# A radix-2 stage of a long convolution taken from TensorE: folds on VectorE and GpSimd, and real and imaginary parts on partitions

## The chip, the cores and the metric

One core of one Trainium2 chip runs the whole kernel. The metric is device time in microseconds. The kernel before takes 373.03 us, the median of 3 runs (372.75 to 373.64).

## The reference

Two branches work on the layer-normalised query `xn` and are added to `x`. Sizes: S = 2048 positions, D = 448 channels, F = 1792.

```python
# A: a 4-tap shift of k, times v, then a causal convolution of length S per channel
k_shift = sum over t of k_pad[:, t:t + S, :] * shift_k[:, 3 - t]
kv = k_shift * v
y = irfft(rfft(pad(kv, 2 * S)) * rfft(pad(ssm_k, 2 * S)))[:S] + kv * ssm_D
A = xn * y
# B: dense -> Mish -> dense
B = mish(xn @ w1 + b1) @ w2
out = x + A + B
```

All operands are fp32. The convolution is computed as a transform in three stages: 64 points with a fold, then 32 points, a product in the frequency domain, and the two stages back.

## The kernel before, in words

**The dense branch is the backbone.** The positions are cut into 8 chunks of 256, the F columns into 7 pairs of 128-wide tiles. Each of the 56 (chunk, pair) steps has two slots. The even slot holds the first product (`g1_mm`, 22 matmuls of 256 columns), the odd slot Mish on ScalarE and its split in two parts on VectorE (`mish`; the tile `acl` is the low part), and the second product (`g2_mm`, 12 matmuls of 448 columns) of the pair two steps back. Layer norm of the next chunk runs beside it: statistics on VectorE in small pieces (`dv` drips one behind another instruction), the normalised rows (`xn`, L391) on GpSimd.

**The transform is laid between the slots by hand.** `at(slot, f)` puts `f` ahead of a slot's dense work, `after(slot, f)` behind it; the lists are run in order of slots, and every engine executes its instructions in the order in which they were written. There is no other scheduler. A DMA is issued by the sequencer of the engine that it is written for, in that engine's order, and what stands behind it on that queue waits as long as it waits.

**Stage 1** (slots 0 to 63) takes 16 groups, 8 of the filter H and 8 of kv: `f1_mm` does 8 matmuls, `f1_fold` adds and subtracts, `f1_out` writes to the DRAM scratch `Dh` or `Dkv`. For kv, `taps` forms the shifted product on VectorE, and one of four multiplications goes to GpSimd (`taps_pool`, L154).

**Stage 2** (slots 63 to 90) takes the frequencies in 8 octets of 8, with three slots to an octet. For octet `o`: `o_load` reads `ah` and `av` from the scratch (one buffer each, so that the load of octet o+1 waits for the matmuls of octet o); `f2_mm` transforms H (`h2_mm`) and kv (`v2_mm`), each with 16 matmuls of a 64-row, 32-column part of the array; ScalarE copies the results out of PSUM (`hs`, `vs`); `prod` multiplies the two complex numbers with six VectorE instructions; `i1_mm` does the first step back with 16 matmuls of a 32-row, 64-column part; ScalarE copies (`qe`) and issues two writes to the scratch `E`. fp32 matmuls are two instructions each, so a view counts 32 where the code has 16.

**Stage 3** (slots 92 to 115) loads `E` by chunks (`e_load`, issued by GpSimd), adds and subtracts halves (`fold`), does the last 8 matmuls of a chunk (`i2_mm`) and gates with the normalised query (`gate`). The first `i2_mm` needs all octets, since every chunk of `E` has rows of every octet. The tables `OCT_AT` and `I2_AT` hold the slots; in stage 2 kv's matmuls stand at 65 + 3 o, H's one slot ahead, `i1_mm` four slots behind.

## Time and profile before

| | |
|---|---|
| median of 3 runs | 373.03 us |
| span of the profiled execution | 370.5 us |
| TensorE busy | 361.2 us, 98% |
| VectorE, ScalarE, GpSimd busy | 261.4, 165.9, 71.2 us |
| DMA traffic | 79.35 MB, 214 GB/s on average |
| stage 2's matmuls (L207 / L250) | 27.9 / 15.8 us of TensorE |

The profile is of one execution, and its span covers the program's instructions from the first to the last; the profiler gives no other time for that execution. The median is 2.5 us above the span. PE is TensorE, PEld its weight loads, DVE VectorE, ACT ScalarE, POOL GpSimd, and SP the queue that issues most loads. A busy TensorE is not one at its peak: matmuls are pipelined, and a part of the array that stands idle doesn't show. The time of a small matmul is read from the distance between its start and the start of what comes behind it.

### The profile page before, as it was taken

Reading aid. Unit: us, or ns where it says so; the run is one execution under the profiler, and the core shown is the slowest. Engines: PE = TensorE matmul, PEld = TensorE weight load, DVE = VectorE, ACT = ScalarE, POOL = GpSimd, SP = SyncE. Lnnn points to the kernel's source line nnn. Section 1 sums busy time; section 2 is a strip of 40 time slices with the busy share of each in tenths; the row PEclk is TensorE's granted clock in tenths of the full one; section 3 lists DMA queues with packets and bytes.
Section 4 is the critical chain, followed back from the end, with each engine's and each line's share of the span. In section 5 each row is a group of like instructions: output and inputs, shape, how many; then the busy total and the mean of one; then the engine's idle time right before and its main releaser. Section 6 shows DMA issues by size and latency. Waiting matters only on the chain.

```text
span 370.5 us, 7467 instructions
## 1 busy us (share of the span) xinstructions
PE 361.2 (98%) x3128; PEld 292.2 (79%) x3128; DVE 261.4 (71%) x358; ACT 165.9 (45%) x277; POOL 71.2 (19%) x59
## 2 busy tenths in 40 slices
PE   8999999999998999999999999999999999999995
PEld 2889888888887988988886666666666879889885
DVE  4899748999968987996435647654474842997751
ACT  2785642343423333343353556555475533235450
POOL 2107002722070223520014000060000005102020
PEclk9999999999999999999999999999999999999999
DMA  8999968757596428504876498988494475949655
GB/s 307 319 308 355 382 233 233 215 159 239 145 294 184 104 58 262 179 25 99 264 235 216 135 282 239 272 271 237 134 328 110 105 239 207 407 195 293 102 69 129
DMA packets 31442, 79.35 MB, mean 214 GB/s; under 512 B 2865, under 2 KB 18098, under 8 KB 31410
## 3 DMA queue, kind: packets, MB, share of 16 engines
q1 hardware_dynamic: 19826, 44.35, 35.4%
q10 hardware_dynamic: 9248, 22.61, 23.0%
q0 software_dynamic: 2336, 11.93, 11.3%
q8 instruction: 24, 0.39, 0.4%
q14 instruction: 8, 0.07, 0.0%
HBM read 50.44 MB, written 28.44 MB: 213 GB/s over the span
## 4 chain that ended last, share of the span: by engine, by line
PE 62%; DVE 4%; ACT 2%; ACTq 1%; issue 1%; DVEq 0%
PE pg L446 24%; PE pg L471 8%; PE pg L473 8%; PE pg L472 8%; PE pc L207 7%; PE pc L250 3%; PE pc L307 2%; PE pc L124 1%; PE pg L406 1%; ACTq L261 1%; ACT a L454 1%; DVE x L171 1%; DVE yc L240 1%; DVE qt L478 0%; ACT XH L418 0%
## 5 line engine op out<-in xcount | busy, mean ns | idle before, releaser
L454 ACT ACTIVATE a<-pg,b1t 128x256 f32<-128x256 f32 x112 | 47.1, 472 | 101.4 <-PE pg L446 80.6
L446 PE MATMUL pg<-XH,w1h 128*128 128x256 f32 x448 | 91.2, 285 | 0.7 <-ACT XH L418 0.7
L446 PEld LDWEIGHTS pg<-XH,w1h 128*128 128x128 f32 x448 | 69.5, 188 | 18.1 <-issue 15.7
L471 PE MATMUL pg<-w2h,ach 128*128 128x448 f32 x224 | 83.0, 371 | 0.0
L472 PE MATMUL pg<-w2l,ach 128*128 128x448 f32 x224 | 81.4, 363 | 0.6 <-DVE w2l L74 0.6
L473 PE MATMUL pg<-w2h,acl 128*128 128x448 f32 x224 | 81.4, 363 | 0.0
L74 DVE TENSOR_TENSOR acl<-a,ach 128x512 fp32r<-128x512 f32 x56 | 38.8, 692 | 55.2 <-ACT ach L73 55.0
L446 PE MATMUL pg<-XL,w1h 128*128 128x256 f32 x448 | 69.6, 277 | 0.0
L446 PEld LDWEIGHTS pg<-XL,w1h 128*128 128x128 f32 x448 | 59.4, 188 | 0.1
L446 PE MATMUL pg<-XH,w1l 128*128 128x256 f32 x336 | 56.9, 278 | 0.0
L471 PEld LDWEIGHTS pg<-w2h,ach 128*128 128x128 f32 x224 | 42.0, 187 | 11.6 <-issue 9.4
L446 PEld LDWEIGHTS pg<-XH,w1l 128*128 128x128 f32 x336 | 46.8, 188 | 0.1
L472 PEld LDWEIGHTS pg<-w2l,ach 128*128 128x128 f32 x224 | 42.1, 188 | 3.5 <-DVE w2l L74 1.1
L473 PEld LDWEIGHTS pg<-w2h,acl 128*128 128x128 f32 x224 | 42.1, 188 | 2.5
L387 POOL TENSOR_TENSOR rstd<-ve,mhalf 128x2 f32<-128x2 f32 (+1 forms) x9 | 8.5, 945 | 162.6 <-DVE ve L384 105.8
L73 ACT CAST ach<-a 128x512 fp32r<-128x512 f32 x56 | 34.7, 620 | 1.8
L154 POOL TENSOR_TENSOR x<-kr,skb 128x896 f32<-128x896 f32 x8 | 17.0, 2129 | 74.9 <-DVE x L153 54.1
L171 DVE TENSOR_TENSOR x<-x 128x896 f32<-128x896 f32 x24 | 26.6, 1107 | 5.1 <-POOL x L154 4.4
L391 POOL TENSOR_SCALAR xn<-qt,mv,rstd 128x448 f32<-128x448 f32 x12 | 26.7, 2231 | 0.6
L418 ACT CAST XH<-pg 128x512 fp32r<-128x512 f32 x16 | 9.4, 587 | 38.7 <-PE pg L406 35.5
L416 DVE TENSOR_TENSOR XL<-pg,XH 128x512 fp32r<-128x512 f32 x16 | 10.9, 687 | 15.5 <-ACT XH L418 15.3
L130 ACT COPY st<-pc 128x896 f32<-128x896 f32 x16 | 14.5, 908 | 14.7 <-PE pc L124 12.8
(71 smaller groups left out, 401.1 us busy)
## 6 DMA issues: line engine op xcount, KB each, us to landing
Dh<-st ACTq DMA_DIRECT2D x16, 448.0 KB, 6.0
Dkv<-st ACTq DMA_DIRECT2D x16, 448.0 KB, 5.1
ah<-Dh SPq DMA_DIRECT2D x8, 896.0 KB, 6.8
av<-Dkv SPq DMA_DIRECT2D x8, 896.0 KB, 5.9
E<-qe ACTq DMA_DIRECT2D x16, 448.0 KB, 5.4
e<-E POOLq DMA_DIRECT2D x8, 896.0 KB, 7.7
kr<-in_k_dram SPq DMA_DIRECT2D x10, 448.0 KB, 6.2
kr<-in_w_dram SPq DMA_DIRECT2D x7, 512.0 KB, 6.3
```

The costliest lines, as they stand in the source:

```text
L73: nc.scalar.copy(h, raw)
L74: V.tensor_sub(l, raw, h)
L130: nc.scalar.copy(st[:, 1], o)
L154: nc.gpsimd.tensor_mul(o, KR[g - u // 2], skb[:, u:u + 1].to_broadcast([128, 2, D]))
L171: V.tensor_add(KV[g], KV[g], o)
L207: nc.tensor.matmul(p[32 * t:32 * t + 32, r, :D], g[rs, t, c], a[rs, t], start=True, stop=True, tile_position=(64 * r, 32 * t))
L391: eng.tensor_scalar(xn[:, jj, :D], Q[c][:, jj], mv[:, j, 0:1], rstd[:, j:j + 1], op0=ALU.subtract, op1=ALU.mult)
L446: nc.tensor.matmul(ps[:, n], l, r, start=n_ == 0, stop=n_ == len(mm) - 1)
L454: nc.scalar.activation(a[:, n], ps[:, n], AF.Mish, bias=b1t[:, 2 * p + n:2 * p + n + 1])
L471: nc.tensor.matmul(ps, ah[:, n, cs], w2h[:, f], start=f == 0, stop=False)
L472: nc.tensor.matmul(ps, ah[:, n, cs], w2l[:, f], start=False, stop=False)
L473: nc.tensor.matmul(ps, al[:, n, cs], w2h[:, f], start=False, stop=f == NF - 1)
```

## The change

Stage 2's 32-point step is cut into a radix-2 stage outside TensorE and two 16-point matmuls.

- **Layout.** A group's results now lie as 32 frequency rows x 2 parts, real and imaginary parts alternating on the partitions. `f1_out` writes four pieces of 32 partitions rather than two of 64, half of them from SP's queue (the last of kv all from ScalarE's). `o_load` reads 2 x 2 x 448 floats to a partition; for octets 4 to 7 (the mirrored frequencies) it exchanges the partitions of the second half, which makes three DMAs of one.
- **`f2_fold`** forms sum and difference of the two halves ahead of the matmuls. kv's folds are on VectorE; H's are on VectorE for octets 0 and 1, on GpSimd from octet 2 on. From octet 4 on the half has a sign by partition: on VectorE this is a `scalar_tensor_tensor`, for GpSimd ScalarE multiplies by the sign first.
- **`f2_mm`** has 16 matmuls as before, each of a 32-row, 32-column part of the array, so that 16 parts rather than 8 are addressed.
- **`h2_turn`** copies H's result from `hs` to `ht` with exchanged partitions, two DMAs of 448 KB on SP's queue.
- **`prod`** has four VectorE multiplications in place (`hs` becomes v times h, `vs` becomes v times the exchanged h), without the sum and the difference: `i1_mm` adds them in its accumulation, with 32 matmuls of 32 x 32 rather than 16 of 32 x 64.
- **`i1_fold`** adds on VectorE and subtracts on GpSimd (both on VectorE for octet 7); **`i1_store`** writes to `E` from SP's queue with four DMAs, from octet 4 on with twelve. Before, ScalarE issued two.
- **`fold`** of stage 3 has four instructions of 448 columns rather than two of 896, two of them `scalar_tensor_tensor`.
- **Slots.** An octet has 3.5 slots on average: kv's matmuls at 66, 70, 73, 77, 80, 84, 87, 91, H's one slot behind those of the octet ahead, `i1_mm` two slots behind kv's. The last `i1_mm` moves from slot 90 to 93, the first `i2_mm` from 98 to 101, the last stays at 110.

```diff
-OCT_AT = (65, 3)
-I2_AT = {98: (6, 7), 102: (0, 1), 106: (2, 3), 110: (4, 5)}
+V_AT = (66, 70, 73, 77, 80, 84, 87, 91)
+I2_AT = {101: (6, 7), 104: (0, 1), 107: (2, 3), 110: (4, 5)}
...
     def f1_out(dst, g, key):
         st = ST.pop((key, g))
+        dst = dst.rearrange("(h k) (r n c) b d -> n c (k r) h (b d)", h=2, r=4, c=2)
         for jj in range(2):
-            nc.scalar.dma_start(dst.rearrange("(h p) n d -> p h n d", h=2)[:, :, 4 * g + 2 * jj:4 * g + 2 * jj + 2].rearrange("p h n d -> p h (n d)"),
-                                st[64 * jj:64 * jj + 64].rearrange("p h b d -> p h (b d)"))
+            for c in range(2):
+                p = 64 * jj + 32 * c
+                (nc.scalar if c or (g, key) == (NO - 1, "kv") else nc.sync).dma_start(dst[2 * g + jj, c], st[p:p + 32].rearrange("p h b d -> p h (b d)"))
...
+    def f2_fold(d, o, name, eng):
+        a = d[o]
+        x = t2([128, 2, D], name)
+        a0, a1 = a[:, :, 0], a[:, :, 1]
+        if o < 4:
+            eng.tensor_add(x, a0, a1)
+            eng is V and dv()
+            eng.tensor_sub(a1, a0, a1)
+            eng is V and dv()
+        elif eng is V:
+            V.scalar_tensor_tensor(x, a1, sg[0], a0, op0=ALU.mult, op1=ALU.add)
+            dv()
+            V.scalar_tensor_tensor(a1, a1, sg[1], a0, op0=ALU.mult, op1=ALU.add)
+            dv()
+        else:
+            nc.scalar.mul(a1, a1, sg[0])
+            eng.tensor_add(x, a0, a1)
+            eng.tensor_sub(a1, a0, a1)
+        d[o] = x, a1
...
+    def f2_mm(d, o):
+        xs = d.pop(o)
         g = GT[o][0]
-        for t in range(4):
-            for r in range(2):
-                rs = slice(64 * r, 64 * r + 64)
-                nc.tensor.matmul(p[32 * t:32 * t + 32, r, :D], g[rs, t, c], a[rs, t], start=True, stop=True,
-                                 tile_position=(64 * r, 32 * t))
-        return p
+        ps = [pc(), pc()]
+        for t in range(2):
+            for e in range(2):
+                for r in range(4):
+                    rs, cg = slice(32 * r, 32 * r + 32), 32 * (2 * t + e)
+                    nc.tensor.matmul(ps[r // 2][cg:cg + 32, r % 2, :D], g[rs, t, e], xs[e][rs, t], start=True, stop=True,
+                                     tile_position=(32 * r, cg))
+        return ps
...
+    def h2_turn(o):
+        HT2[o] = t2([128, 4, D], "ht")
+        for c in range(2):
+            nc.sync.dma_start(HT2[o][c::2], HS[o][1 - c::2])
...
+    def prod(o):
+        v, h, ht = PV[o], HS[o], HT2.pop(o)
+        for x, y in ((h, h), (v, ht)):
+            for i in range(2):
+                hf = slice(2 * i, 2 * i + 2)
+                V.tensor_mul(x[:, hf], v[:, hf], y[:, hf])
+                dv()
...
+    for o, s in enumerate(V_AT):
+        h = V_AT[o - 1] + 1 if o else H0_AT
+        before = V_AT[o - 2] + 1 if o > 1 else H0_AT
+        at(before if o else h - 3, o_load, AH, Dh, o, "ah")
+        at(V_AT[o - 1] if o else s - 3, o_load, AV, Dkv, o, "av")
+        after(h - 2, f2_fold, AH, o, "xh", V if o < 2 else nc.gpsimd)
         at(h, h2_mm, o)
-        after(h, h2_out, o)
+        at(h, h2_out, o)
+        at(h + 1, h2_turn, o)
+        after(s - 2, f2_fold, AV, o, "xv", V)
         at(s, v2_mm, o)
-        after(s, v2_out, o)
+        at(s, v2_out, o)
         at(s, gi_load, o)
-        after(s + 1, prod, o, 0)
-        after(s + 2, prod, o, 1)
-        at(s + 4, i1_mm, o)
-        after(s + 4, i1_out, o)
+        after(s, prod, o)
+        at(s + 2, i1_mm, o)
+        at(s + 2, i1_out, o)
+        after(s + 2, i1_fold, o, (V, nc.gpsimd) if o < 7 else (V, V))
+        at(s + 4, i1_store, o)
```

Where the change puts the new instructions is seen in three places of the engines' order. In these rows the line numbers are each kernel's own.

GpSimd in stage 2, before: the layer norm of the last chunks (L387 to L395), and behind it at once stage 3's loads of `E`.

```order
L387 TENSOR_TENSOR rstd<-ve,mhalf 128x2
L391 TENSOR_SCALAR xn<-qt,mv,rstd 128x448 x2
L395 COPY xn<-xn 128x2x64
L387 TENSOR_TENSOR rstd<-ve,mhalf 128x2
L283 DMA e_3448<-E 128x2x896
```

GpSimd at the same place now, octets 2 to 4 of H (L215, L217, L226, L227 are `f2_fold`, L291 is `i1_fold`).

```order
L444 COPY xn<-xn 128x2x64
L291 TENSOR_TENSOR qe<-ie,qe 128x2x448
L215 TENSOR_TENSOR xh<-ah 128x896
L217 TENSOR_TENSOR ah<-ah 128x2x448
L291 TENSOR_TENSOR qe<-ie,qe 128x2x448
L215 TENSOR_TENSOR xh<-ah 128x896
L217 TENSOR_TENSOR ah<-ah 128x2x448
L291 TENSOR_TENSOR qe<-ie,qe 128x2x448
L226 TENSOR_TENSOR xh<-ah 128x896
L227 TENSOR_TENSOR ah<-ah 128x2x448
L436 TENSOR_TENSOR rstd<-ve,mhalf 128x2
L440 TENSOR_SCALAR xn<-qt,mv,rstd 128x448 x2
```

Each fold of H on GpSimd now stands behind the `i1_fold` of two octets back.

SP's queue in the second half of stage 2, before: tables (`g`, `gi`) and loads of `ah` and `av`.

```order
L191 DMA g<-in_c_g_dram 128x256
L194 DMA ah<-Dh 128x4x448
L198 DMA gi<-in_c_gi_dram 128x256
L194 DMA av<-Dkv 128x4x448
L365 DMA qt<-in_q_dram 128x896
```

SP's queue now, from the end of the store of octet 4 (the two rows of L301 and L303 stand there four times) to the loads of `av` for octet 6 and `ah` for octet 7.

```order
L301 DMA E<-qe 32x2x448
L303 DMA E<-qe 16x2x448 x2
L207 DMA gi<-in_c_gi_dram 128x256
L201 DMA av<-Dkv 128x2x448
L203 DMA av<-Dkv 64x2x448 x2
L414 DMA qt<-in_q_dram 128x896
L194 DMA g<-in_c_g_dram 128x128
L201 DMA ah<-Dh 128x2x448
L203 DMA ah<-Dh 64x2x448 x2
L253 DMA ht<-hs 64x1792 x2
```

The loads of `av` and `ah` and the exchange `ht` now stand behind twelve stores on one queue.

VectorE in the second half of stage 2, before: the six instructions of one octet's product with the splits (`acl`) between.

```order
L240 TENSOR_TENSOR ya<-vs,hs 128x896
L240 TENSOR_TENSOR yb<-vs,hs 128x896
L240 TENSOR_TENSOR ya<-ya,yb 128x896
L74 TENSOR_TENSOR acl<-a,ach 128x512
L240 TENSOR_TENSOR yc<-vs,hs 128x896
L240 TENSOR_TENSOR yd<-vs,hs 128x896
L240 TENSOR_TENSOR yc<-yc,yd 128x896
```

VectorE now, around the product of octet 5 (L268).

```order
L291 TENSOR_TENSOR qe<-ie,qe 128x2x448
L220 SCALAR_TENSOR_TENSOR xv<-av,f1id 128x896
L222 SCALAR_TENSOR_TENSOR av<-av,f1id 128x2x448
L75 TENSOR_TENSOR acl<-a,ach 128x512
L268 TENSOR_TENSOR hs<-vs,hs 128x896 x2
L268 TENSOR_TENSOR vs<-vs,ht 128x896 x2
L75 TENSOR_TENSOR acl<-a,ach 128x512
```

Four products, two folds of kv and one of the step back stand where six instructions of the product stood.

More of the change, by code (lines that the diff above doesn't have):

```diff
@@ L51, in tile_kernel @@
     dp = pool("scratch", space=DRAM)
-    Dh = dp.tile([NO * 16, 32, D], F32, name="Dh")
-    Dkv = dp.tile([NO * 16, 32, D], F32, name="Dkv")
-    E = dp.tile([NJ * 4, 64, D], F32, name="E")
+    Dh = dp.tile([NO * 2, 128, 2, D], F32, name="Dh")
+    Dkv = dp.tile([NO * 2, 128, 2, D], F32, name="Dkv")
+    E = dp.tile([NJ * 32, 8, D], F32, name="E")
     f1id = cp.tile([128, 2, 128], F32, name="f1id")
     f1, ident = f1id[:, 0], f1id[:, 1]
+    sg = [f1id[:, 0, 64 + i:65 + i] for i in range(4)]
     mhalf = cp.tile([128, 2], F32, name="mhalf")
@@ L211, in h2_mm @@
+    def f2_mm(d, o):
+        xs = d.pop(o)
+        g = GT[o][0]
+        ps = [pc(), pc()]
[6 more added lines that the diff above has]
+        return ps
     def h2_mm(o):
-        PS["H", o] = [f2_mm(AH[o], o, c) for c in range(2)]
@@ new lines, in i1_fold, with i1_store @@
+    def i1_fold(o, engs):
+        e, y = QE[o]
+        for i, f in enumerate(engs):
+            (f.tensor_sub if i else f.tensor_add)(y[:, :, i], e, y[:, :, 1])
+            f is V and dv()
+    def i1_store(o):
+        h, k = divmod(o, 4)
+        y = QE.pop(o)[1]
+        dst = E.rearrange("(x o r) (t h b) d -> o h r x t b d", o=4, r=4, h=2, b=2)[k, h]
+        for r in range(4):
+            fr, to = y[32 * r:32 * r + 32], dst[r]
+            if h:
+                nc.sync.dma_start(to[:, :, 0], fr[:, :, 0])
+                for c in range(2):
+                    nc.sync.dma_start(to[1 - c::2, :, 1], fr[c::2, :, 1])
+            else:
+                nc.sync.dma_start(to.rearrange("x t b d -> x t (b d)"), fr.rearrange("x t b d -> x t (b d)"))
```

140 lines of the change are left out of this document (67 added, 73 removed).

## The prediction

> **What bounds the kernel now.** I read the page's busy shares first, then the chain that ended last, then stage 2 alone by stretches, and last the groups and single tiles that the change touches.
>
> ```profile
> span 370.5 us, 7467 instructions
> PE 361.2 (98%) x3128; PEld 292.2 (79%) x3128; DVE 261.4 (71%) x358; ACT 165.9 (45%) x277; POOL 71.2 (19%) x59
> ...
> PE 62%; DVE 4%; ACT 2%; ACTq 1%; issue 1%; DVEq 0%
> ```
> ```profile
> core 0: us, PE busy (x) PEld busy (x) DVE busy (x) ACT busy (x) POOL busy (x), PEclk, DMA share, GB/s
> 184.00:290.00 106.00, 104.77 (x1165) 71.37 (x1150) 58.66 (x69) 58.38 (x89) 11.64 (x8) 1.00 0.72 218
> ```
>
> TensorE is the bound, at full granted clock. In stage 2 (184 to 290) it idles 1.23 of 106 us, while GpSimd works 11.6 us. VectorE has 47 us to spare, the DMA engines are 72% busy. So whatever leaves TensorE here is gained in full, and whatever makes it wait is paid in full.
>
> ```profile
> 213.52 2.72 PE pg L446 x22
> 216.24 1.66 PE pc L207 x32
> 217.90 0.40 PE pg L471
> ...
> 220.51 1.69 PE pc L250 x32
> 222.21 2.69 PE pg L446 x22
> ```
>
> These pieces of the chain give a slot's price: a first product 2.7 us, a second (217.90 to 220.51) 2.6, a transform of one octet 1.66, a step back 1.69.
>
> **The matmuls.**
>
> ```profile
> 216.17 0.18 PEld L207 LDWEIGHTS pc<-av,g 64*32 64x32 f32 x16
> 216.57 0.15 PEld L207 LDWEIGHTS pc<-av,g 64*32 64x32 f32 x8 [0.22 <-issue]
> 216.95 0.15 PEld L207 LDWEIGHTS pc<-av,g 64*32 64x32 f32 x8 [0.22 <-issue]
> 217.83 0.47 PE L471 MATMUL pg<-w2h,ach 128*128 128x448 f32 x1
> ```
>
> The 32 instructions go in four rounds of eight, one every 0.38 us; within a round the loads start together (eight within 0.15 us), so that the busy array and not the issue sets the round. With 32 x 32 parts sixteen fit in a round. Two rounds go: 1.66 - 2 x 0.38 = 0.90, and eight more starts cost some 0.05, so 0.95. Gain 0.71 x 16 = **11.4 us**. No row has sixteen parts at once: at worst the gain is 0. I take the whole, since eight starts fit easily in 0.38. `i1_mm` keeps four rounds (64 instructions, sixteen at a time): 0. The 1.23 us of old idle time goes too, its waits being replaced by those below: **-1.2**.
>
> **The loop of H on GpSimd.** One `ah` buffer makes a ring: H's matmuls, load of the next `ah`, fold, next matmuls.
>
> ```profile
> L194 SPq DMA_DIRECT2D ah<-Dh x8: 359/370/525, 177.2 to 266.6; - x8
> DMA to landing us min/median/max: 4.9/6.8/8.1
> L154 POOL TENSOR_TENSOR x<-kr,skb x8: 2113/2132/2136, 62.6 to 164.3; 128x896 f32<-128x896 f32 x8
> 220.45 1.01 PE L250 MATMUL pc<-ya,gi 32*64 32x448 f32 x16
> 222.25 1.72 ACT L258 COPY qe<-pc 128x896 f32<-128x896 f32 x2 [2.87 <-PE pc L250]
> ```
>
> A GpSimd instruction on 896 columns is 2.13 us, and the step back's copies end 3.5 us after its matmuls start (220.45 to 223.97). Where H's matmuls follow after three slots (octets 3, 5, 7) TensorE needs from the end of one to the start of the next: slots 2.6 + 2.7 + 2.6, a step back 1.7, kv's transform 0.95: 10.6 us. On octet 3, GpSimd first subtracts for octet 1. With H's end at 0, that step back starts after 2.6, its copies end at 6.1, three GpSimd instructions end at 12.6 (0.1 for the hand-over): wait **2.1**. On octets 5 and 7 the load takes three issues (about 0.4 each) and 6.8: landed at 7.7; ScalarE's multiplication, a fold of 4.3 and Mish ahead of it on ScalarE bring 12.9: **2.3**. With four slots there are 13.2 us, and octet 4 waits 0, octet 6 **0.45** (Mish comes last).
>
> **SP's queue.** Twelve stores from octet 4 on.
>
> ```profile
> 299.05 0.80 SPq L298 DMA_DIRECT2D q<-in_q_dram  x2
> 2.58 0.45 SPq L598 DMA_DIRECT2D b1t<-in_b_dram  x1
> ```
>
> An issue is 0.4 us even for 7 KB, so twelve hold the queue 5 us, and `av` of octet 6, `ah` of octet 7 and the exchange of octet 7 stand behind them. `av` 6 is issued some 2.5 us late, lands after 6.3 and is folded by VectorE in 2.7 (two of 1.35, from twice a 0.68 row of 448 columns): it comes **2.2** late; `ah` 7 then lacks **0.9** instead of its 2.3. At the stage's end kv 7 waits **0.8** (its fold stands behind octet 6's `i1_fold`), and the exchange of octet 7, behind octet 5's stores, lands some 4 us after kv's copies could have started the product, which overwrites `hs` and so must wait for it: step back 7 waits **2.6**. In the other octets the exchange (6.8 from the landing row above) has 9.8 us and hides.
>
> ```profile
> L318 DVE SCALAR_TENSOR_TENSOR q<-q,mv,pc 128x448 f32<-128x448 f32 x10 | 6.3, 676 | 2.3 <-PE pc L307 2.3
> ```
>
> **Start and end of the stage.**
>
> ```profile
> 185.77 0.38 SPq L194 DMA_DIRECT2D av<-Dkv  x1
> 190.69 1.74 PE L207 MATMUL pc<-av,g 64*32 64x448 f32 x32
> ```
>
> The first `av` was issued at 185.8, as soon as `Dkv` had landed, and used at 190.7. Now ScalarE issues four pieces rather than two (1.2 us later) and a fold of 2.1 stands between, against one slot more less 0.7 saved: wait **1.6**.
>
> ```profile
> 297.88 1.01 PE pc L250 x16
> ...
> 319.90 1.24 PE pc L307 x17
> ```
> ```profile
> 300.67 1.25 ACTq L261 DMA_DIRECT2D E<-qe  x2
> 318.56 1.09 DVE L291 TENSOR_TENSOR e<-e 128x896 f32<-128x896 f32 x1
> ```
>
> From the last step back to stage 3's first matmuls there are 22.0 us with no slack at the end (the last fold ends at 319.65). Both versions leave eight slots. New in it: `i1_fold` 2.2, stores 0.3 to 2.6 (twelve issues are 5 us against 1.25, but small pieces land sooner), two longer folds 0.9; some 1 us of slack ahead of the first fold goes against it. Wait 2.4 to 4.6: **3.0**.
>
> **What is hidden.** Stage 1's SP writes wait for a fold with k and v loads behind them; these loads are early (GpSimd and VectorE, not DMA, time the taps), so 0, and up to 1 us if a load came late. VectorE has six product instructions less two, plus three: 1.1 us more an octet, within its 47 us. Stage 3's closer slots have 26 us of VectorE work in 29. Queues keep their order elsewhere.
>
> **GpSimd and VectorE side by side.** Stage 2 had nearly no GpSimd work; now both read SBUF all the time.
>
> ```profile
> 194.86 3.92 POOL L391 TENSOR_SCALAR xn<-qt,mv,rstd 128x448 f32<-128x448 f32 x2
> 195.22 1.49 DVE L240 TENSOR_TENSOR ya<-ya,yb 128x896 f32<-128x896 f32 x1
> 145.47 5.00 POOL L391 TENSOR_SCALAR xn<-qt,mv,rstd 128x448 f32<-128x448 f32 x2
> L391 POOL TENSOR_SCALAR xn<-qt,mv,rstd x12: 1855/2130/3148, 29.5 to 245.0; 128x448 f32<-128x448 f32 x12
> 75.64 2.12 POOL L154 TENSOR_TENSOR x<-kr,skb 128x896 f32<-128x896 f32 x1 [3.89 <-DVE x L153]
> 76.54 1.09 DVE L133 TENSOR_TENSOR st<-pc,st 128x896 f32<-128x896 f32 x1
> ```
>
> Two `xn` take 3.71 undisturbed (2 x 1.855), but 3.92 and 5.00 beside VectorE instructions with two SBUF operands, one of which took 1.49 rather than 1.09. The 2.13 us of L154 was measured only beside folds that read PSUM (L133), so it may be too low. An octet has four products, two folds, an `i1_fold` and 1.75 splits: 8.8 us of such VectorE work in 12.9, so 68% of GpSimd's 6.4 us, 4.4 us, meet it. By the rows GpSimd loses 0.2 to 0.35 us per us met; bounds are 0 and 1. I take 0.3: 1.3 us an octet, 6.5 over five folds, and half of it in waits that GpSimd ends: **3.5** (0 to 13.8).
>
> The Trainium skill, "SBUF — State Buffer", section "Who interferes with whom", goes further: a VectorE instruction with two SBUF inputs and a GpSimd instruction that reads SBUF exclude each other for a whole instruction. The trace disagrees in part, as the 1.49 us instruction ended inside the `xn` that it met. By the page's rule the sum would be that of the second rival.
>
> **Sum.** -11.4 - 1.2 + 2.1 + 2.3 + 0.45 + 2.2 + 0.9 + 0.8 + 2.6 + 1.6 + 3.0 + 3.5 = +6.9: span 377.4, and with the 2.5 us between the span and the median shown (373.03), **380 us**.
>
> **Rivals.**
>
> First, faster: GpSimd adds two plain operands in 1.45 us (no row has that form). Then three instructions end at 10.6, the waits of octets 3 and 5 and the 3.5 vanish, 7.9 in all: 372.0, and with half a microsecond saved at octet 6 371.5. Below 1.45 us it decides. For it: L154 has a broadcast operand; against it: that operand costs VectorE nothing. If SP's queue and the loads are kinder too (4.9 us to land), the 6.5 us of its waits go: 365.
>
> Second, exclusion: VectorE 8.8 + GpSimd 6.4 = 15.2 us an octet against 12.9, 2.3 x 6 = 13.8 in place of the 3.5 and of the 4.85 at octets 3, 5, 6: 385.
>
> Third, the transfers become the bound. An octet moves 3.67 MB rather than 2.75 with the exchange; 218 GB/s at 72% scales to 96%. Loads would land at the row's 8.1 rather than 6.8, 1.3 us in four turns of the loop: 385.
>
> Fourth, sixteen parts don't run at once: 391.
>
> **How the numbers follow.** Less than 0.2% can't be told from no change. Forecast 0.38, second 0.15, third 0.11, fourth 0.04: slower 0.68. First rival 0.17 and its kinder form 0.09: faster 0.26, with 0.06 for waits that just cancel the gain. The range 365 to 389 leaves out the fourth and the ends of the others; the forecast's own is 375 to 385.
>
> **What would show it.** L207's successor with 0.95 us from start to the next piece; TensorE waiting for GpSimd's folds of `ah` ahead of H's matmuls, for VectorE's of `av` around octet 6, for the product ahead of the last step back, and for `e` at stage 3; GpSimd instructions on 896 columns above 2.13 us; DMA share above 0.9 in stage 2. I am wrong if GpSimd's are at 2.1 or less and no stretch of stage 2 has TensorE idle for more than a few tenths.

## The result, and the profile after

The changed kernel takes **433.85 us** (median; 431.62 to 436.36), against 372.9 us of the kernel before (372.75 to 373.64): 1.164 times the time, 95% interval 1.159 to 1.169, 61 us slower. The forecast was 380 us with a range of 365 to 389: the sign was right, the size far off. The profiled execution spans 434.6 us against 370.5. Below, runs 1, 4 and 7 each hold one slower execution (420.6, 391.3 and 417.4 us; run 1's profile is of it), which counts in their medians and ranges and not in their ratios.

The head of the page, and the chain's shares by engine:

```profile
span 434.6 us, 8298 instructions
PE 382.1 (88%) x3384; PEld 299.0 (69%) x3384; DVE 302.6 (70%) x387; ACT 169.3 (39%) x281; POOL 119.9 (28%) x78
...
PE 33%; DVE 12%; DMA 10%; SPq 5%; ACT 5%; issue 4%; POOL 4%; ACTq 0%; DVEq 0%; POOLq 0%
```

TensorE lost on two accounts. It idles 434.6 - 382.1 = 52.5 us (before: 9.3), and it is busy 20.9 us longer, although its new matmuls should take less. The stretches of stages 2 and 3 show why:

```profile
core 0: us, PE busy (x) PEld busy (x) DVE busy (x) ACT busy (x) POOL busy (x), PEclk, DMA share, GB/s
190.00:210.00 20.00, 19.88 (x228) 14.95 (x226) 13.41 (x15) 10.91 (x18) 2.61 (x3) 1.00 0.81 281
210.00:232.00 22.00, 18.54 (x237) 11.57 (x236) 16.98 (x12) 9.58 (x14) 13.05 (x6) 1.00 0.77 246
232.00:260.00 28.00, 18.41 (x184) 12.04 (x185) 13.76 (x14) 8.28 (x12) 8.16 (x4) 0.76 0.58 164
260.00:282.00 22.00, 16.22 (x222) 9.76 (x220) 18.74 (x14) 8.06 (x12) 16.99 (x7) 0.88 0.70 211
...
325.00:350.00 25.00, 14.10 (x155) 9.88 (x154) 8.06 (x11) 5.57 (x10) 2.07 (x1) 0.80 0.43 122
```

In the worst stretches (232 to 260, 325 to 350) every engine idles for a third of the time or more, and the DMA share is lower than before (0.72), so neither an engine nor the transfers are full: something stands in line. The granted clock there is 0.76 and 0.80, so that the matmuls between the waits are slow too.

The timeline of the changed kernel around the first of them (start, length, engine, what; in brackets the idle time before and what ended it), in the order of the chain:

```profile
226.70 0.38 SPq L199 DMA_DIRECT2D av<-Dkv  x1
237.45 0.34 SPq L532 DMA_DIRECT2D out_dram<-qt  x1
237.88 3.04 SPq L305 DMA_DIRECT2D E<-qe  x4
...
229.96 2.45 POOL L217 TENSOR_TENSOR ah<-ah 128x896 f32<-128x896 f32 x1
...
230.39 3.96 DVE L268 TENSOR_TENSOR hs<-vs,hs 128x896 f32<-128x896 f32 x2
...
236.28 1.14 DVE L527 TENSOR_TENSOR qt<-pg,qt 128x448 f32<-128x448 f32 x2
...
245.11 0.91 ACT L286 COPY qe<-pc 128x896 f32<-128x896 f32 x1 [4.43 <-DMA E<-qe]
...
247.44 0.69 DVE L75 TENSOR_TENSOR acl<-a,ach 128x512 fp32r<-128x512 f32 x1 [10.02 <-ACT ach L74]
250.12 2.70 DVE L215 TENSOR_TENSOR xv<-av 128x896 f32<-128x896 f32 x1
...
252.96 1.72 PE L238 MATMUL pc<-xv,g 32*32 32x448 f32 x8 [8.06 <-DVE mv L430]
```

This is one chain. SP's queue does nothing from 227.1 to 237.45: it holds the output write of chunk 4, which waits for VectorE's evacuation (L527, to 237.4), which stands behind a product that GpSimd slowed (the first two multiplications took 3.96 us beside the fold of L217, and 1.09 each where nothing met them). Behind the write stand the stores of octet 1; ScalarE's copy into the single `qe` waits for them to land; Mish stands behind that copy on ScalarE; VectorE's `acl` waits for Mish, 10 us; kv's fold stands behind `acl`; and TensorE waits 8.06 us for the fold. The same chain comes again ahead of kv's matmuls of octet 7: 10.90 us.

### The profile page after: what moved, and what is told of

It reads as the page before. It is cut to its first block, busy times and chain, and to the rows that moved or that the text cites. A ratio compares the mean times of both kernels' runs of the same rounds, so it can differ in the third digit from the quotient of the medians.

```text
span 434.6 us, 8298 instructions
## 1 busy us (share of the span) xinstructions
PE 382.1 (88%) x3384; PEld 299.0 (69%) x3384; DVE 302.6 (70%) x387; ACT 169.3 (39%) x281; POOL 119.9 (28%) x78
## 4 chain that ended last, share of the span: by engine, by line
PE 33%; DVE 12%; DMA 10%; SPq 5%; ACT 5%; issue 4%; POOL 4%; ACTq 0%; DVEq 0%; POOLq 0%
PE pg L495 12%; PE pg L520 5%; PE pg L521 4%; PE pg L522 4%; PE pc L238 3%; DMA ht<-hs 3%; SPq L303 2%; DMA ah<-Dh 2%; DVE av L217 2%; DMA e<-E 2%; DMA E<-qe 1%; DVE qe L291 1%; PE pc L279 1%; DMA Dkv<-st 1%; PE pc L356 1%
## 5 line engine op out<-in xcount | busy, mean ns | idle before, releaser
L75 DVE TENSOR_TENSOR acl<-a,ach 128x512 fp32r<-128x512 f32 x56 | 42.7, 762 | 67.1 <-ACT ach L74 67.0
L520 PE MATMUL pg<-w2h,ach 128*128 128x448 f32 x224 | 85.6, 382 | 3.2 <-DVE qt L527 2.8
L521 PE MATMUL pg<-w2l,ach 128*128 128x448 f32 x224 | 83.2, 371 | 0.8 <-DVE w2l L75 0.8
L522 PE MATMUL pg<-w2h,acl 128*128 128x448 f32 x224 | 82.7, 369 | 0.0
L520 PEld LDWEIGHTS pg<-w2h,ach 128*128 128x128 f32 x224 | 43.3, 193 | 17.6 <-issue 13.9
L521 PEld LDWEIGHTS pg<-w2l,ach 128*128 128x128 f32 x224 | 43.5, 194 | 3.9 <-DVE w2l L75 1.4
L291 POOL TENSOR_TENSOR qe<-ie,qe 128x896 f32<-128x896 f32 x7 | 16.9, 2416 | 91.0 <-DVE qe L291 52.3
L238 PE MATMUL pc<-xv,g 32*32 32x448 f32 x128 | 15.9, 646 | 20.1 <-DVE mv L430 19.0
L440 POOL TENSOR_SCALAR xn<-qt,mv,rstd 128x448 f32<-128x448 f32 x12 | 28.9, 2415 | 0.6
L268 DVE TENSOR_TENSOR hs<-vs,hs 128x896 f32<-128x896 f32 x16 | 26.2, 1673 | 0.0
```

Source lines behind the costliest of these rows:

```text
L75: V.tensor_sub(l, raw, h)
L238: nc.tensor.matmul(ps[r // 2][cg:cg + 32, r % 2, :D], g[rs, t, e], xs[e][rs, t], start=True, stop=True, tile_position=(32 * r, cg))
L268: V.tensor_mul(x[:, hf], v[:, hf], y[:, hf])
L291: (f.tensor_sub if i else f.tensor_add)(y[:, :, i], e, y[:, :, 1])
L440: eng.tensor_scalar(xn[:, jj, :D], Q[c][:, jj], mv[:, j, 0:1], rstd[:, j:j + 1], op0=ALU.subtract, op1=ALU.mult)
L520: nc.tensor.matmul(ps, ah[:, n, cs], w2h[:, f], start=f == 0, stop=False)
```

## The experiments

The edits are against the changed kernel, where nothing else is said. "Folds" are `f2_fold` and `i1_fold`.

**1. All folds on VectorE.**

```diff
-        after(h - 2, f2_fold, AH, o, "xh", V if o < 2 else nc.gpsimd)
+        after(h - 2, f2_fold, AH, o, "xh", V)
-        after(s + 2, i1_fold, o, (V, nc.gpsimd) if o < 7 else (V, V))
+        after(s + 2, i1_fold, o, (V, V))
```

> All folds of H and all of the step back's sums on VectorE: GpSimd has no work left in stage 2 but layer norm's, and ScalarE's multiplications by the sign go. VectorE gets some 19 instructions of 1.1 us more, 21 us. Theory E (exclusion of GpSimd and VectorE instructions is the root): VectorE's products are back at 1.1 us each instead of up to 2.95, the waits ahead of the folds go, TensorE's idle time in stage 2 (36 us in the changed kernel) falls below 15, time 390 to 408. Theory Q (the order of SP's queue is the root: an output write that waits for VectorE, with stores, the load of H and the exchange behind it): the two long waits ahead of kv's matmuls of octets 3 and 7 (8.1 and 10.9 us) stay at 5 or more each, time 415 to 432.

415.9 us (412.5 to 420.6), ratio 1.111 (1.104 to 1.118): 18 us off, although VectorE does more. The gain is theory E's in kind, but smaller (415.9 against at most 408). The time is at the edge of theory Q's range, and the two long waits ahead of kv's matmuls of octets 3 and 7 stayed, 9.15 and 13.16 us, as theory Q had it. Both causes were there.

**2. Output writes later.**

```diff
         if not late(c):
-            nc.sync.dma_start(out[:, 2 * c:2 * c + 2], x)
+            if c in (4, 5):
+                at(14 * c + 21, nc.sync.dma_start, out[:, 2 * c:2 * c + 2], x)
+            else:
+                nc.sync.dma_start(out[:, 2 * c:2 * c + 2], x)
```

> The changed kernel, but the output writes of chunks 4 and 5 stand three slots further back on SP's queue, behind the stores, loads and exchanges that they held up. Nothing else. Theory Q: the stores of octets 1 and 5 leave some 8 us earlier, ScalarE's copies of qe don't wait for them, the waits of 8.1 and 10.9 us ahead of kv's matmuls of octets 3 and 7 fall below 4 each; time 412 to 422. Theory E: VectorE and GpSimd stay late by themselves, the two waits keep at least 6 us each; time 428 to 435.

422.1 us (421.7 to 425.2), ratio 1.132 (1.127 to 1.138). The place of two writes on a queue is worth 11.8 us. The waits of 8.06 and 10.90 us became 3.54 each, below 4 as theory Q had it; the time is 0.1 us above its range.

**3. The price of GpSimd's company, in the kernel before.**

```diff
+    def probe(o):
+        for _ in range(3):
+            nc.gpsimd.tensor_add(sp2[0].tile([128, 2, D], mybir.dt.bfloat16, name="pa", bufs=1), HS[o][:, 0], HS[o][:, 1])
...
+        if o:
+            after(s, probe, o)
```

> The kernel before, with three GpSimd additions of 896 columns (both inputs from hs in SBUF) in each octet from 1 on, whose result nobody reads: 21 instructions, some 45 us of GpSimd work beside VectorE's six products an octet, and nothing waits for them but the next use of hs. The price of the company alone. Theory E: instructions exclude each other strictly, so that VectorE's products reach 2.9 us where they meet and GpSimd's mean is 2.6 or more; VectorE loses up to 45 us in stage 2 against 47 us to spare, so TensorE waits: time 380 to 395. Theory Q: exclusion is there but is absorbed as long as no queue hangs on it: time 373 to 378.

384.6 us (383.7 to 387.7), ratio 1.032 (1.026 to 1.038): 11 us for 21 instructions whose result nobody reads. The groups of the probe and of VectorE's products (mean ns last before the second bar), then the products in the kernel before:

```profile
L231 POOL TENSOR_TENSOR pa<-hs 128x896 bf16<-128x896 f32 x21 | 57.2, 2724 | 31.1 <-ACT hs L218 29.9
L244 DVE TENSOR_TENSOR yc<-yc,yd 128x896 f32<-128x896 f32 x8 | 19.4, 2427 | 0.2
```
```profile
L240 DVE TENSOR_TENSOR yc<-yc,yd 128x896 f32<-128x896 f32 x8 | 8.7, 1090 | 0.2
```

The worst of the six instructions of a product takes 2.43 us rather than 1.09 on average; the other five stand between 1.09 and 1.80. VectorE is busy 293.8 us rather than 261.4: 32.4 us for 21 instructions, 1.5 us each, and GpSimd loses 0.6 us each itself (a mean of 2.72 against the shortest, 2.11). The time lies in theory E's range; the kernel pays a third of VectorE's loss. That the rest fell into VectorE's spare time is the likely reading, not a measured one.

**4. The matmuls and layouts alone.**

```diff
-        after(h - 2, f2_fold, AH, o, "xh", V if o < 2 else nc.gpsimd)
-        at(h + 1, h2_turn, o)
-        after(s - 2, f2_fold, AV, o, "xv", V)
-        after(s + 2, i1_fold, o, (V, nc.gpsimd) if o < 7 else (V, V))
...
-        xs = d.pop(o)
+        a = d.pop(o)
+        xs = a[:, :, 0], a[:, :, 1]
...
-        for x, y in ((h, h), (v, ht)):
+        for x, y in ((h, h), (v, v)):
...
-        for x, p in zip((e, y[:, :, 1]), PS.pop(("I", o))):
+        for x, p in zip((y[:, :, 0], y[:, :, 1]), PS.pop(("I", o))):
```

> The changed kernel without its folds of H and kv, without the exchange and without the sums of the first step back: the transforms multiply the raw halves, the products take v times v in the second half, ScalarE copies straight into the tile that is stored. Left are the sixteen-part matmuls, the new layouts with all their loads and stores (twelve small ones from octet 4 on), the new slots. Both theories: matmuls 0.95 us for an octet's transform. Theory E: no GpSimd work, no folds, so nothing is late: time 359 to 367, 6 to 14 below the kernel before. Theory Q: the output write that waits, and stores of 0.6 us an issue, hold SP's queue by themselves: TensorE idle 5 us or more in stage 2, time 368 to 385.

389.9 us (385.4 to 391.3), ratio 1.039 (1.029 to 1.048), above the ranges of both theories: without any fold, the kernel is still slower than before. Where nothing waits, a transform takes 0.96 us (247.97 to 248.93) as forecast; but a step back takes 2.07, against 1.69 before:

```profile
247.97 1.03 PE L239 MATMUL pc<-ah,g 32*32 32x448 f32 x32
...
248.93 0.62 PE L496 MATMUL pg<-XH,w1h 128*128 128x256 f32 x3
...
251.63 1.03 PE L280 MATMUL pc<-hs,gi 32*32 32x448 f32 x32
252.41 1.36 PE L280 MATMUL pc<-vs,gi 32*32 32x448 f32 x32
253.70 0.47 PE L521 MATMUL pg<-w2h,ach 128*128 128x448 f32 x1
```

The chain is there too: ScalarE's copy into `qe` waits 10.80 us for the stores behind the output write, and TensorE 2.98. What follows the wait runs at half clock, for 6.5 us:

```profile
239.95 1.71 ACT L287 COPY qe<-pc 128x896 f32<-128x896 f32 x2 [10.80 <-DMA E<-qe]
```
```profile
240.91 2.60 PE L239 MATMUL pc<-av,g 32*32 32x448 f32 x32 [2.98 <-ACT qe L287]
```
```profile
core 0: us, PE busy (x), PEclk, DMA share, GB/s
232.60:237.90 5.30, 5.30 (x42) 1.00 0.71 205
240.90:244.40 3.50, 3.49 (x35) 0.50 0.95 279
244.40:248.00 3.60, 3.60 (x16) 0.55 0.83 221
248.00:252.00 4.00, 4.00 (x71) 1.00 0.96 300
```

The transform took 2.53 us instead of 0.96 and the second product behind it 4.53 instead of 2.6: a wait of 3.0 costs another 3.5.

**5. Runs 1 and 2 together.**

> The edits of the first two runs together: all folds on VectorE, and the output writes of chunks 4 and 5 three slots later on SP's queue. Apart they took 18 and 12 us off the changed kernel's 434. Theory Q+E (two causes, each worth its own): the waits ahead of kv's matmuls of octets 3 and 7 fall below 2 each and the short waits for GpSimd are gone; the gains add, time 400 to 406. Theory V (VectorE becomes the bound: 4 products, 4 fold instructions and 2 sums of 1.09 us, and the split of acl, come to some 12.5 us in an octet of 3.5 slots that takes 12.9): new waits of TensorE for VectorE take part of it back, time 407 to 414.

404.1 us (404.0 to 404.3), ratio 1.085 (1.084 to 1.087): the gains add, as theory Q+E had it (the waits at octets 3 and 7 stayed at 3.0 and 6.0, where it had them below 2). Between runs 2 and 5 only the engine of the folds and sums differs, VectorE instead of GpSimd: **18.0 us**. Their groups from 195 to 340 us, run 2 first:

```profile
L268 DVE TENSOR_TENSOR hs<-vs,hs 128x896 f32<-128x896 f32 x15 | 23.2, 1587 | 0.0
L75 DVE TENSOR_TENSOR acl<-a,ach 128x512 fp32r<-128x512 f32 x14 | 15.4, 1103 | 29.6 <-ACT ach L74 29.6
L226 POOL TENSOR_TENSOR xh<-ah 128x896 f32<-128x896 f32 x4 | 10.9, 2715 | 0.0
```
```profile
L268 DVE TENSOR_TENSOR hs<-vs,hs 128x896 f32<-128x896 f32 x16 | 16.8, 1090 | 0.0
L75 DVE TENSOR_TENSOR acl<-a,ach 128x512 fp32r<-128x512 f32 x17 | 11.7, 690 | 30.6 <-ACT ach L74 30.6
```

What was left at octet 7 is SP's queue again, this time by the stores themselves: twelve issues from 295.30 to 303.67, 0.7 us each, and ScalarE's copy for octet 6 waits until they have landed.

```profile
295.30 0.54 SPq L301 DMA_DIRECT2D E<-qe  x1
...
302.48 1.19 SPq L303 DMA_DIRECT2D E<-qe  x2
```
```profile
306.70 0.91 ACT L286 COPY qe<-pc 128x896 f32<-128x896 f32 x1 [2.95 <-DMA E<-qe]
```

**6. The matmuls alone, output writes later** (the edits of 4 and 2).

> The kernel with the matmuls alone (no folds, no exchange, no sums), now with the output writes of chunks 4 and 5 three slots later. It had waits of 3.0 and 7.0 us where ScalarE's copy into qe waited for a store that stood behind the output write, each followed by a transform and a second product that took 3.5 us longer at a lower clock. Theory Q: both go with their clock loss, some 17 us: time 371 to 375, with transforms 0.96 and steps back 2.06 us, and stage 3's wait for VectorE (2.8 us at L528) left. Against Q: the twelve stores hold the queue by themselves, the 7.0 us of octet 7 stay at 4 or more: time 378 to 385.

380.8 us (378.7 to 382.7), ratio 1.023 (1.018 to 1.027). The time is inside the range of the case against Q: 9 us rather than 17 went. The wait is not as that case had it: the 7.0 us of octet 7 became 3.36 rather than 4 or more, now ahead of its step back, which waits for its coefficients `gi`, loaded behind the same stores.

**7. Output writes later, four stores an octet.**

```diff
-            if h:
+            if False:
                 nc.sync.dma_start(to[:, :, 0], fr[:, :, 0])
```

> The changed kernel with the output writes later, as in the second run, and with four stores to E for every octet, rather than twelve from octet 4 on. It leaves out the exchange of the partitions in the stored second half for these octets. Everything else stays. If the twelve issues matter by themselves (I had put 5 us of SP's queue, and 6.5 us of TensorE's waits, on them), the waits at octets 6 and 7 (3.5 us ahead of kv's matmuls of octet 7 in the second run, 3.0 inside its step back's start) fall, time 408 to 417. If they only showed because the output write had held them up, 419 to 424.

413.8 us (410.5 to 417.4), ratio 1.110 (1.101 to 1.120), against 422.1 in run 2: the twelve stores cost some 8 us by themselves, as the first case had it. The waits were not quite as that case named them: 2.18 us ahead of octet 6's kv and 2.13 at stage 3's start fell to nothing and to 0.20, but octet 7's kv still waited 3.53. This run leaves out the exchange of the stored halves.

**8. The matmuls alone, with second buffers** (the edits of run 6 and these).

```diff
-        QE[o] = e, y = t2([128, 2, D], "ie"), t2([128, 2, 2, D], "qe")
+        QE[o] = e, y = None, t2([128, 2, 2, D], "qe", 2)
...
-        gi = t2([128, 4, 2, 32], "gi")
+        gi = t2([128, 4, 2, 32], "gi", 2)
...
-        at(s, gi_load, o)
+        at(s - 1, gi_load, o)
...
-            after(t - 4 + m if n else t - 3 + m, fold, c)
+            after(t - 2 + m if n == 1 else t - 4 + m if n else t - 3 + m, fold, c)
```

> The sixth run (matmuls alone, output writes later) with a second buffer for qe and for gi, the load of gi one slot earlier, and stage 3's folds for chunks 0 and 1 two slots later, behind VectorE's evacuation of chunk 6. It leaves out the folds, the exchange and the sums. Theory Q (what is left in the sixth run comes from single buffers behind stores of 0.6 us an issue, and from the order on VectorE): the wait of 3.4 us ahead of octet 7's step back goes, and that of 2.8 us at the evacuation, each with its clock loss; transforms save 0.70 x 16 = 11.3, steps back cost 0.37 x 8 = 3.0; time 367 to 372, below the kernel before. If the stores or the layouts cost by themselves (DMA traffic, landings), 375 or more.

375.1 us (375.0 to 378.0), ratio 1.009 (1.006 to 1.012), theory Q's 367 to 372 missed: the waits of 3.36 and 2.8 us went, the clock is at 0.999, and still it is not faster. How far it had come is read from the start of the same Mish: slot 96, when stage 2's work is done in both, and slot 110. In the kernel before, then in this one:

```profile
317.54 0.84 ACT L454 ACTIVATE a<-pg,b1t 128x256 f32<-128x256 f32 x2 [2.01 <-DVE XL L416]
...
359.40 0.84 ACT L454 ACTIVATE a<-pg,b1t 128x256 f32<-128x256 f32 x2 [0.22 <-PE pg L446]
```
```profile
314.52 0.84 ACT L504 ACTIVATE a<-pg,b1t 128x256 f32<-128x256 f32 x2 [2.01 <-PE pg L496]
...
363.22 0.82 ACT L504 ACTIVATE a<-pg,b1t 128x256 f32<-128x256 f32 x2
```

At slot 96 it is 3.0 us ahead, of 8.3 that the matmuls save (11.3 on the transforms, less 8 x 0.37 on the steps back). The rest went in a wait for layer norm's `xn` (2.0) and inside four steps back, whose second products came late (5 us by the trace); the kernel before has 1.2 us of idle time there itself. The wait for `xn` is the company of GpSimd and VectorE once more: two `xn` took 5.89 us beside the products, against 3.92 in the kernel before. At slot 110 it is 3.8 behind: stage 3 costs 6.8 us. VectorE is busy 25.69 of 27 us there, and two pairs of last matmuls take 3.7 and 5.0 us rather than 1.66, waiting inside for a fold:

```profile
321.00:348.00 27.00, 26.71 (x192) 19.15 (x191) 25.69 (x42) 6.56 (x13) 3.08 (x5) 1.00 0.86 309
```

**9. No exchange** (run 5 without `h2_turn`, second product v times v).

> The fifth run (all folds on VectorE, output writes later) without the exchange of H by DMA: the second product takes v times v. It leaves out the exchange alone. If the exchange (two DMAs an octet on SP's queue, and a product that waits for them) is part of the 23 us between the fifth and the sixth run, the waits ahead of the steps back and at octet 7 shrink and the time falls to 390 to 398. If these 23 us are VectorE's folds and sums, which stand in the way of Mish's split and of one another, it stays at 400 to 405.

401.0 us (400.3 to 403.4), ratio 1.078 (1.074 to 1.082): the exchange of H costs some 3 us, and is not where the 23 us between runs 5 and 6 are.

**10. Run 5 with stores on two queues**, and stage 3's folds moved as in run 8.

```diff
+        eng = (nc.sync, nc.gpsimd)[part]
...
-        for r in range(4):
+        for r in (2 * part, 2 * part + 1):
...
-        at(s + 4, i1_store, o)
+        at(s + 4, i1_store, o, 0)
+        at(s + 3, i1_store, o, 1)
```

> The fifth run with half of the stores to E on GpSimd's queue one slot earlier (GpSimd has no other work there), and stage 3's folds for chunks 0 and 1 two slots later, behind the evacuation of chunk 6. The whole computation. Theory Q: SP's queue is held 3.5 rather than 8 us by octet 5's stores, ScalarE's copy of octet 6 doesn't wait, the 6.0 us ahead of kv's matmuls of octet 7 fall below 2 and the 2.7 at the evacuation go, with their clock losses: time 388 to 394. Theory V (VectorE): the wait of octet 7 moves to VectorE's folds and sums, time 396 to 403. Neither expects it to beat the kernel before.

391.5 us (390.2 to 391.9), ratio 1.050 (1.047 to 1.053), within theory Q's range: 12.6 us for the two edits. The wait at octet 7 fell from 6.0 to 3.05, not below 2.

**11 and 12. Stage 3's last matmuls further apart**, for the matmuls alone (run 8) and the whole computation (run 10).

```diff
-I2_AT = {101: (6, 7), 104: (0, 1), 107: (2, 3), 110: (4, 5)}
+I2_AT = {101: (6, 7), 105: (0, 1), 109: (2, 3), 112: (4, 5)}
```

> The eighth run (matmuls alone, second buffers) with stage 3's last matmuls at slots 101, 105, 109 and 112 rather than 101, 104, 107 and 110, its folds moved along. It leaves out the folds of H and kv, the exchange and the sums of the step back. Up to slot 86 the eighth run was 7.0 us ahead of the kernel before, and 3.8 behind at slot 110. Theory S (stage 3's closer slots cost it: four fold instructions a chunk make VectorE the bound for 26 us, TensorE waits inside two of the last matmuls): with an average of 3.7 slots between them the waits go, time 368 to 372, below the kernel before. If the loss there comes from E landing late, the first of these matmuls keeps its 2 us and the time stays at 373 to 376.

> The tenth run (all folds on VectorE, output writes later, stores on two queues; the whole computation) with the same slots for stage 3's last matmuls. Theory S: its two waits inside them (2.9 and 3.4 us) go, time 385 to 389. If the landing of E sets stage 3's start, 389 to 392. By either it stays 12 us or more behind the kernel before: the waits ahead of kv's matmuls of octets 3 and 7 (3 us each and the clock behind them) stay, since VectorE's fold of kv stands behind the split of Mish there.

380.2 us (378.2 to 380.7), ratio 1.021 (1.019 to 1.022), and 394.6 us (393.8 to 396.5), ratio 1.060 (1.057 to 1.063): both slower than what they came from, a miss for every theory. The waits in stage 3 did shrink, but the last output writes now end the kernel. Run 8 issued the last of GpSimd's at 363.61 us, run 11 at 367.41, where TensorE ends at 368.1 and the write lands only at 374.8. The clock took its part too: behind the same wait of 2.01 us for `xn` it fell to 0.50 for some 3.3 us in run 11, and stayed at 1.00 in run 8. How the 5 us divide was not measured.

**13. The same with the last at slot 110** (101, 105, 108, 110; matmuls alone).

> The eleventh run with stage 3's last matmuls at slots 101, 105, 108 and 110: wider where TensorE waited, and the last where it was, since the last output writes of the eleventh run landed 7 us after TensorE's end. It leaves out the folds of H and kv, the exchange and the sums of the step back. If stage 3's spacing is the cause of the eighth run's loss there, two waits inside the last matmuls go and nothing is lost at the end: time 370 to 373, level with the kernel before or a little faster. If the waits only move to the matmuls at 108 and 110, it stays at 374 to 377.

379.3 us (377.2 to 381.7), ratio 1.015 (1.009 to 1.021): the waits moved to the last pair, as the second case had it, at 2 us more than its range. TensorE waits there for the gate, behind VectorE's folds, for a PSUM buffer:

```profile
358.22 0.57 PE L357 MATMUL pc<-ex,i 64*32 64x448 f32 x2 [1.24 <-DVE q L368]
...
362.21 0.96 PE L357 MATMUL pc<-ex,i 64*32 64x448 f32 x2 [3.00 <-DVE q L368]
```

**14. kv's fold ahead of the sums of the octet before** (run 10 with VectorE's order changed).

```diff
         after(s - 2, f2_fold, AV, o, "xv", V)
+        if o:
+            after(V_AT[o - 1] + 2, i1_fold, o - 1, (V, V))
+        if o == NO - 1:
+            after(s + 2, i1_fold, o, (V, V))
...
-        after(s + 2, i1_fold, o, (V, V))
```

> The tenth run (whole computation, folds on VectorE, output writes later, stores on two queues) with one order changed: VectorE does kv's fold ahead of the sums of the step back of the octet before. Theory order: the waits of 3.1 us ahead of kv's matmuls of octets 3 and 7 go, with the half clock behind them (1.9 and more each); time 380 to 385. Theory amount: VectorE has that much to do in any order, the waits move to the octets' other folds or to the stores; time 388 to 392.

392.9 us (391.8 to 396.0), ratio 1.054 (1.048 to 1.061), no gain, as theory amount had it within a microsecond: the waits of 3.1 us for kv's fold fell to 0.4 (with 0.5 more inside the transforms), and three for `gi` came, whose load now stands behind stores that wait for later sums:

```profile
222.43 1.81 PE L279 MATMUL pc<-hs,gi 32*32 32x448 f32 x32 [2.67 <-DMA gi<-in_c_gi_dram]
```

**15. Run 14 with the slots of run 13.**

> The fourteenth run with stage 3's last matmuls at slots 101, 105, 108 and 110 as well: the whole computation with every cause mended that the runs have shown. Theory order: 377 to 382. Theory amount: 385 to 390. Neither expects it to beat the kernel before (372.6), since the matmuls alone with all else mended are level with it.

397.6 us (395.5 to 398.2), ratio 1.064 (1.059 to 1.070): outside both. The waits of run 13 are there with the same lengths, 1.24 and 3.00 us ahead of the last pair.

**16. Run 14 with the load of `gi` off SP's queue.**

```diff
-        nc.sync.dma_start(gi, c_gi[:, o])
+        nc.gpsimd.dma_start(gi, c_gi[:, o])
...
-        at(s, gi_load, o)
+        if not o:
+            at(s, gi_load, o)
...
+        if o + 1 < NO:
+            at(s + 2, gi_load, o + 1)
```

> The fourteenth run (whole computation; folds on VectorE, kv's fold ahead of the sums, output writes later, stores on two queues) with the load of gi on GpSimd's queue, issued as soon as the step back before has read its buffer. Theory order: the three waits of 2.7, 1.4 and 2.5 us ahead of the steps back go, with the half clock behind them (1.3, 0 and 2.0): time 381 to 385. Theory amount: other waits for VectorE take their place, time 388 to 393.

387.8 us (387.4 to 388.3), ratio 1.042 (1.040 to 1.044), between the two theories, and the best that does the whole computation. The clock is back at 0.997; the longest wait ahead of a matmul is 1.82 us. What is left stands inside the transforms. In TensorE's and VectorE's timelines, the second half of the matmuls waits for the fold's second instruction:

```profile
238.46 0.95 PE L238 MATMUL pc<-xv,g 32*32 32x448 f32 x8 [0.39 <-DVE xv L215]
239.90 0.58 PE L238 MATMUL pc<-av,g 32*32 32x448 f32 x4 [0.48 <-DVE av L217]
...
240.84 0.47 PE L521 MATMUL pg<-w2h,ach 128*128 128x448 f32 x1
```
```profile
237.24 1.08 DVE L215 TENSOR_TENSOR xv<-av 128x896 f32<-128x896 f32 x1
...
238.77 1.07 DVE L217 TENSOR_TENSOR av<-av 128x896 f32<-128x896 f32 x1
```

This transform takes 2.38 us (238.46 to 240.84) rather than 0.96. Eleven of the sixteen transforms are late in this way, by 0.4 to 1.5 us each and 11.7 us in all by the trace, from a transform's start to the next piece. Between the medians of runs 16 and 8 lie 12.7 us; run 8 has late steps back of its own, so the two numbers need not be the same thing.

**Where the 61 us went**, by differences of medians: 11.8 the place of two output writes (changed kernel to run 2); 18.0 GpSimd's share of the folds (to run 5); 12.6 the stores on one queue and stage 3's order on VectorE, not told apart (to run 10); 3.7 the order of kv's fold and of `gi`'s load (to run 16); 12.7 folds, sums and exchange on VectorE, with stores and buffers that differ a little (to run 8); 2.5 the rest, the matmuls' gain included (to the kernel before). The order of the edits matters little for the first two: run 1 alone took 17.9 us off, run 2 alone 11.8, both together 29.8. No version beat the kernel before.

## Why the prediction was wrong

The direction was right: TensorE waits for folds, loads and stores. Three steps of the sum failed: SP's queue (6.5 us of waits in the sum), GpSimd beside VectorE (3.5, and 13.8 at most), and a clock that falls behind each long wait (not in the sum). Two smaller terms failed too: the step back (0 in the sum, 3.0 in the runs) and stage 3 (3.0, and some 7 more in the changed kernel).

- **f2 matmuls, -11.4: right.** 0.96 us where nothing waits; the sixteen parts run at once, and the fourth rival falls.
- **`i1_mm`, 0: wrong, +3.0.** A step back takes 2.06 rather than 1.69 us in the runs without folds, 0.37 x 8. By run 4's rows its first half, on `hs`, takes 0.78 us (251.63 to 252.41), two rounds of 0.39; the second, which adds `vs` onto it, takes 1.29 (to 253.70). Why was not tested.
- **The loop of H.** Octet 3 waits 2.4 (forecast 2.1), octets 4 and 6 nothing (0 and 0.45), octet 7 3.4 (0.9 in the sum, as kv of octet 6 was to be late; 2.3 without that), octet 5 5.8 (2.3). The ring is as forecast. At octet 5 GpSimd's three instructions took 8.6 us rather than 6.4, and began 3.3 us after the copies (271.95 against 268.63): layer norm held GpSimd until 270.26, and its subtraction, which overwrites an input of VectorE's sum, had to wait for that sum, until 271.81. The forecast let GpSimd start when the copies end.
- **GpSimd and VectorE side by side, 3.5 (0 to 13.8): the term failed**. Moving the folds and sums away from GpSimd was worth 18.0. That also holds the loop of H, so it stands against the 3.5 and the 4.85 of octets 3, 5 and 6, or against the bound of 13.8 that was to replace both; it is above the bound too. "By the rows GpSimd loses 0.2 to 0.35 us per us met" was read from `xn`, a TENSOR_SCALAR; a GpSimd TENSOR_TENSOR holds up VectorE's two-input instructions much longer (2.43 us rather than 1.09 in run 3, up to 2.99 in the changed kernel), and both engines lose. `xn` itself lost more here than the rows said: two took 6.68 us (263.23 to 269.91) rather than 3.71, beside 5.0 us of such VectorE work, so some 0.6 us per us met, an estimate from this trace. The bound set the two engines' work end to end against the length of an octet; it had no term for what stands behind a late VectorE on other engines and queues. The Trainium skill, "SBUF — State Buffer", section "Who interferes with whom", has the rule that I weighed down to 0.15: it calls the port pair that the two engines share an exclusive lock, for which a VectorE instruction with two SBUF inputs contends with a GpSimd instruction that reads SBUF. The trace agrees for these instructions: 2.70 rather than 1.08 for kv's fold (250.12, in the changed kernel), a mean of 2.72 rather than 2.1 for GpSimd's addition (run 3).
- **SP's queue: the step that failed most.** The sum had 6.5 us. The place of two output writes was worth 11.8, and the stores on one queue, together with stage 3's order, 12.6. "An issue is 0.4 us even for 7 KB" was 0.7 for these stores (twelve in 8.4 us), and "Queues keep their order elsewhere" missed that an output write, which waits for VectorE, stood ahead of the stores, and that ScalarE's copy into a single `qe` waits for stores to land, with Mish behind it. I had named what stands behind the stores on SP, but not who waits for a store to have landed. Two waits of 8.06 and 10.90 us came of it, ahead of kv of octet 3 (forecast 0) and octet 7 (forecast 0.8). Octet 6's kv waited 1.1 rather than 2.2 (its two fold instructions took 1.15 us each, not 1.35), step back 7 1.1 rather than 2.6, likely since octet 7 was late anyhow; kv of octets 1 and 5 waited 1.5 and 1.6 inside their transforms, which I had not counted.
- **The clock: a term that was missing.** Every wait was counted at its length. In the changed kernel the mean granted clock is 0.948; TensorE's busy time should have fallen by 8.3 us (11.3 less 3.0) and rose by 20.9. As an estimate from that mean, the missing 0.052 of the clock is some 22 us of the 434.6; run 4 shows 3.5 us behind one wait.
- **Start and end of the stage.** Stage 3's first matmuls wait 3.1 (forecast 3.0). But that pair then takes 5.96 us rather than 1.66, and TensorE waits 2.8 more for VectorE's evacuation behind it, some 7 us that were not in the sum: "26 us of VectorE work in 29" was right (25.69 in 27 in run 8), and I called it hidden; there two pairs of matmuls waited inside for a fold, 2.0 and 3.3 us. The first kv has no wait to speak of, but loses 1.0 inside its transform (forecast 1.6).
- **The rivals.** The second (exclusion) had the right mechanism and 13.8 us, 5.4 more than the terms it replaced, where the runs show 18.0. The third falls: in stage 2 the DMA share is 0.42 to 0.81, mostly below that of before (0.72). The first falls: GpSimd's additions on 896 columns took 2.4 to 2.7 us on average, and none less than 2.07.

## What to carry to other kernels

Where a change moves writes or loads onto a queue, list for each what stands ahead of it and what that waits for, and who waits for it to *land*: with single buffers, one late evacuation travels through a store, a copy and an activation to TensorE. When TensorE is the bound, price a wait at its length and add what the lower clock costs behind it (here 1.6 to 3.5 us for each wait above 2.4). Before giving work to GpSimd beside a busy VectorE, measure the pair: here both engines paid. A fold that VectorE finishes just too late delays the matmuls by up to its own length: here 0.4 to 1.5 us, where a transform gained 0.7.

## What the hardware showed that was not expected

Behind a long wait of TensorE the granted clock is 0.50, whatever ended the wait. Each of the 39 single waits of 2.39 us or more in the traces of the changed kernel and of the runs was followed, within 3 us, by such a stretch, mostly of 3 to 6.6 us, with 1.6 to 3.5 us lost; waits below 1 us that stood alone, past the kernel's first 15 us, left it at 1.00. Between 1.5 and 2.4 us it went either way: a wait of 1.54 us was followed by half clock (run 14), waits of 2.18 (run 2) and 2.34 (run 1) were not. Here is the same wait, at the same place, in runs 6 and 8, and the clock behind it (the number behind POOL's count):

```profile
200.72 0.33 PE L456 MATMUL pg<-f1id,xn 128*128 128x128 f32 x1 [2.01 <-POOL xn L445]
...
200.70:204.50 3.80, 3.78 (x12) 3.38 (x13) 1.38 (x2) 1.94 (x4) 0.00 (x0) 0.55 0.47 190
```
```profile
199.57 0.33 PE L456 MATMUL pg<-f1id,xn 128*128 128x128 f32 x1 [2.01 <-POOL xn L445]
...
199.57:203.40 3.83, 3.83 (x59) 2.87 (x69) 1.38 (x2) 1.95 (x4) 0.00 (x0) 1.00 0.55 215
```

The Trainium skill, "TensorE: Matmul & The Clock Gate", section "Part 1: The HAM clock gate (the "warmup" mystery)", tells of half clock after an idle window of about 3.4 us that runs freely. The trace agrees in the half, and in that the same wait of 2.01 us met it or not; but shorter waits than that window were enough here (2.01 us in run 6), and the half clock lasted up to 6.5 us behind a single wait in run 4.
